# A finer, reordered work list for the convolution rounds of an S4 + SwiGLU block

## The chip, the cores and the metric

The kernel runs on one core of a Trainium2 chip. The metric is the device time of one execution in microseconds (us). The core has five engines that run their own instruction streams in order and wait for one another through semaphores: TensorE (PE, matrix products into PSUM), VectorE (DVE), ScalarE (ACT), GpSimd (POOL) and SyncE (SP, which here only issues DMA transfers). ACT and POOL issue DMA transfers too.

## The reference

The input x is 2048 rows of 640 numbers. A modulation vector (silu(c) @ w_mod) gives shifts, scales and gates. Two stages follow, each on a layer-normed and modulated copy h of x and each added back to x with a gate:

- A state-space convolution. For each of 640 channels a kernel of 2048 taps is built, K[d, l] = Re sum over n of C·exp(dt·A·l)·dt·B with 128 complex states n, and h is convolved with K causally (the reference does it with a padded FFT); Dskip·h is added.
- A SwiGLU: h @ w1 through silu, times h @ w3, all times w2, with 1728 hidden columns.

Everything is fp32.

## The kernel before, in words

**Stages.** The time falls into a front (modulation, first layer norm, first transform of u, up to about 120 us), the convolution rounds (to about 317 us), a tail of the convolution (to about 366 us), and the SwiGLU (the rest).

**The work of the rounds.** It is cut into pieces, each a small function that issues a few instructions. A piece is named by two letters and a step number, as in `T+2`. Two families run beside each other.

*Making K*: a step k makes 16 of the 640 channels, so there are 40 steps, 0 to 39.
`PH` phases as integers (three POOL operations, two steps at once), `AB`, `CO`, `SI` absolute value, cosine and sine on ACT (two steps at once), `PA` and `PQ` the exponents (PE), `XA` and `XQ` their exponentials (ACT), `E1`, `E2`, `A1`, `A2` the products of exponentials with cosines and sines (DVE, tiles E and A), `kg` the sum over the states (64 small matmuls into PSUM tile pk), `K` two DVE operations: one adds D to a column of pk (`pk<-pk,dz`), one scales pk by the gate and moves it to SBUF (`K<-pk,gaT`); `pt` a first transform of K (PE), `uk` its copy to SBUF (ACT).

*Convolving*: a step takes 4 of 32 frequencies of 128 channels (5 chunks of channels, 8 steps each). Its steps are numbered 10 to 49, so that step k of this family is worked on in the round of step k of the other.
`st` the second transform of u and K together (16 matmuls into PSUM tile p2, `p<-uk,s`), `kc` the copy of K's half (ACT), `T` two DVE products of the complex multiplication: one into an SBUF tile (`T<-p,kc`), one back into p2 (`p<-p,kc`); `Y` the difference and the sum of the products (DVE), `iv` the first inverse transform (PE, tile pz), `zt` its copy out and store (ACT and SP, every second step).

**What sets the order.** Inside the rounds every instruction of PE, DVE, ACT and POOL is held in the order in which the program issues it. That order is a string, `ROUND` (line 1028), of pieces with steps relative to the round; the loop of line 1037 goes through it for ten rounds of four steps (`EB` = 4), skipping what is done or does not exist. `do` (line 927) finds the function of a piece. A round also has, in rounds 2 to 6, one part of a late modulation product (`LS`, `LP`, `LC`, `LO`, PE and DVE). After the rounds a loop (line 1058) does the remaining convolution steps, from `st` 43 on.

DMA issues on SP are not held in that order, but SP takes them one after the other: a transfer behind one that waits is late too. The loads concerned are `s2` (in traces `s<-in_s_dram`, 256 KB, one per convolution step, two buffers), `i1`, the u of the next chunk (`uk<-us`), the stores `zs<-zt`, and, in the last rounds, `last_pair`: s2 and i1 of the last four steps, put into phase tiles that are free by then (`ph<-in_s_dram`).

**Buffers that make the pieces wait.** p2 has one PSUM place (a second one only for odd steps from 39 on), so `st` of a step waits for `Y` of the step before. PA and PQ share one place, so they alternate with XA and XQ. pk, pt and pz have one each. Phase tiles have three places: `PH` of a step waits until `A1` and `A2` of the six and five steps before it are done. The cosine tiles have two places: `AB` waits for `E1` and `E2` of four and three steps before.

Of the kernel before, what the change touches and what calls it, by code (L numbers as in the profile page):

```python
# [13 lines left out]
OP = mybir.AluOpType  # L14
# [3 lines left out]
P = 128  # L18
L = 2048
D = 640  # L20
F = 1728
NA, NB = 32, 64
DC = 128
# [3 lines left out]
NS = D // SD  # L27
EB = 4
# [13 lines left out]
def consts():  # L42
# [78 lines left out]
def tile_kernel(ctx: ExitStack, tc: tile.TileContext, a):  # L121
    nc = tc.nc
    V, S, G, PE = nc.vector, nc.scalar, nc.gpsimd, nc.tensor
# [51 lines left out]
    dz = kp.tile([P, D // 4], F32, name="dz")  # L175
# [4 lines left out]
    uk = kp.tile([P, 3, NA, DC], F32, name="uk")  # L180
# [261 lines left out]
    def late_load(i):  # L442

        late[i] = w_load(xw[:, :KD * WC].rearrange("p (k c) -> p k c", k=KD), 1920 + i * WC)
# [108 lines left out]
    ph, cs, AA, EC, PK, K1 = {}, {}, {}, {}, {}, {}  # L553
# [16 lines left out]
    def exp_slow(steps):  # L570
        exponents(pQ, steps, r1, NA)
# [65 lines left out]

    def imag2(s):
        A = AA[s]
        keep(V.scalar_tensor_tensor(A[:, :, 0, :], ph.pop(s)[:, :, 2 * NA - 1:NA - 1:-1], -1.0, A[:, :, 0, :],  # L640
                                    op0=OP.mult, op1=OP.mult))

    def tables(s):
# [3 lines left out]
    def kgen(s):  # L647
# [6 lines left out]
                                   start=(st == 0), stop=(st == 1), tile_position=(0, dq * 32)))  # L654
        PK[s] = pk

    def k1evac(s):
        dst = tp.tile([P, SD // 4, NB], F32, name="K1")
        pk = PK.pop(s)
        keep(V.tensor_tensor(pk[:, :, 0], pk[:, :, 0], dz[:, s * 4:s * 4 + 4], op=OP.add))  # L660
        keep(V.tensor_tensor(dst, pk, bc(gaT[:, s * 4:s * 4 + 4], 2, NB), op=OP.mult))
        K1[s] = dst

# [15 lines left out]
    Pq, Yq, Zq = {}, {}, {}  # L679
# [60 lines left out]
    def products(ch, g):  # L740

        p2, kc = Pq[ch, g]
        T = fp.tile([P, 2, 2, DC], F32, name="T")
        T2 = p2[:, :, :, DC:]
        keep(V.tensor_tensor(T, bc(p2[:, :, 0, :DC], 2, 2), kc, op=OP.mult))
        keep(V.tensor_tensor(T2, bc(p2[:, :, 1, :DC], 2, 2), kc[:, :, ::-1, :], op=OP.mult))
        Pq[ch, g] = (T, T2)

    def sums(ch, g):
        T, T2 = Pq.pop((ch, g))  # L750
        Y = fp.tile([P, 2, 2, DC], F32, name="Y")
        keep(V.tensor_tensor(Y[:, :, 0, :], T[:, :, 0, :], T2[:, :, 0, :], op=OP.subtract))
        last_sum[0] = keep(V.tensor_tensor(Y[:, :, 1, :], T[:, :, 1, :], T2[:, :, 1, :], op=OP.add))
        Yq[ch, g] = Y
# [101 lines left out]
    def x_tile():  # L856
        return xp.tile([P, D], F32, name="xm", bufs=6)
# [22 lines left out]
    def x_load(j):  # L880
        xe.append(xw[:, j * D:(j + 1) * D])
        nc.sync.dma_start(xe[j], a["x"][j * P:(j + 1) * P, :])
# [33 lines left out]
    def conv_part(fn):  # L916
        return lambda k: fn((k - LAG) // 8, (k - LAG) % 8)

    parts = {"PH": phases, "AB": absph, "CO": cosine, "SI": sine, "PA": lambda k: exp_fast((k,)), "XA": fast,
             "PQ": lambda k: exp_slow((k,)), "XQ": slow, "E1": real1, "E2": real2, "A1": imag1, "A2": imag2,  # L920
             "kg": kgen, "K": k1evac, "pt": k_stage1, "uk": k_out}
    conv = {"st": conv_part(stage2), "kc": conv_part(k_copy), "T": conv_part(products), "Y": conv_part(sums),
            "iv": conv_part(inverse1), "zt": conv_part(z_store)}
    by_two = ("PH", "AB", "CO", "SI")
    done = set()
# [1 line left out]
    def do(name, k):  # L927

        lo, hi = (LAG, LAG + 8 * NDC) if name in conv else (0, NS)
        if name in by_two and k % 2:  # L930
            return None
        if front[0]:
            assert (name, k) not in done and lo <= k < hi, (name, k)
        if (name, k) in done or not lo <= k < hi or (name == "zt" and k % 2 == 0 and k < LAG + 8 * NDC - 8):
            return None
        done.add((name, k))
        return (conv if name in conv else parts)[name](k)
# [72 lines left out]
    for word in FRONT:  # L1010
        name, k = word[:2].rstrip("+"), int(word[len(word[:2].rstrip("+")):])
# [14 lines left out]
    front[0] = False  # L1026

    ROUND = (
# [5 lines left out]
    ).split()  # L1034
    in_order[0] = True
    pieces = {"LS": late_sums, "LP": late_part, "LC": late_cols, "LO": late_out}
    for rnd in range(NS // EB):
        if 2 <= rnd < 7:
            late_load(rnd - 2)
        for word in ROUND:  # L1040
            name, k = word[:2].rstrip("+-"), EB * rnd + int(word[len(word[:2].rstrip("+-")):])
            if name in pieces:
                if 2 <= rnd < 7:
                    pieces[name](rnd - 2)
                continue
            do(name, k)
            if name == "iv" and 36 <= k < 40:
                with tc.issue_after(i1_last[0].ins):
                    last_pair(k - 36)
            if name == "E1" and 30 <= k < 38 and k % 2 == 0:  # L1050
                x_load((k - 30) // 2)

            if name == "kg" and 36 <= k < 40:
                early.append((None, z_tile()))
                z_load(early[-1][1], k - 36, range(3), q=nc.gpsimd)
    in_order[0] = False

    for tk in range(NS + 1, LAG + 8 * NDC + 2):
        do("st", tk)
        do("kc", tk)  # L1060
        if tk == LAG + 8 * NDC:
            end, made = late_products(6), []
            for j in (2, 3):
                py, end = x_products(j, end)
                made.append(py)
            with tc.issue_after(end.ins):
                last = do("iv", tk - 1)
        else:
            last = do("iv", tk - 1)
        do("zt", tk - 1)  # L1070
        do("T", tk)
        do("Y", tk)
        if tk == NS + 1:
            tabs.close()
            xp = ctx.enter_context(tc.tile_pool(name="xp", bufs=2))
            idle = xp.tile([P, 512], F32R, name="idle", bufs=1)
            G.memset(idle.bitcast(F32), 0.0)
            for j in range(4):
                early[j] = (x_tile(), early[j][1], xp.tile([P, KD, 6], F32, name="st5", bufs=4))
                G.memset(early[j][1][64:, :, 2 * DC:], 0.0)  # L1080
            i2bt = [h_tile() for _ in range(8 - LATE)]
        i = tk - 1 - LAG - 8 * NDC + 8
        if 0 <= i < 8:
            if i < 4:
                z_last_load = z_load(early[i][1], i, (3,), q=nc.gpsimd)
            if i == 3:
                with tc.issue_after(z_last_load.ins):
                    for t in range(8 - LATE):
                        for j in range(4):
                            nc.gpsimd.dma_start(i2bt[t][j * 32:j * 32 + 8], a["i2b"][:, t])  # L1090
            if i in (4, 5):
                x_part(i - 4, x_products(i - 4, last)[0])
            if i == 7:
                for j in (2, 3):
                    x_part(j, made[j - 2])
            if i == 6:
                pl = psS.tile([P, 2, 512], F32, name="pl", tag="A", bufs=1)
                pls += [pl[:, 0], pl[:, 1]] + [psS.tile([P, 512], F32, name="pl", tag=t, bufs=1) for t in ("pk", "pb")]
                late_products(5)
            if i == 7:  # L1100
                z_early()
                early_products()
                late_products(7)
# [22 lines left out]
    V, S, G, PE = (InOrder(tc, e, (in_order,)) for e in (nc.vector, nc.scalar, nc.gpsimd, nc.tensor))  # L1126
# [128 lines left out]
    def x_sums(i, which=range(4)):  # L1255
# [450 lines left out]
```

## Time and profile before

| | us |
|---|---|
| median of 3 runs | 929.97 |
| lowest, highest | 929.65, 930.44 |
| the profiled execution's own time | 929.82 |
| its span, first to last instruction | 927.9 |
| the T of steps 10, 14, 18, 22, 26, 30 and 34 starts at | 128.22, 155.31, 182.38, 209.45, 236.54, 263.63, 290.82 |
| the st of step 42 starts at | 335.02 |
| the last matmul of the convolution's tail ends at | about 366.2 |

The rows below are of four kinds. A row of the windows gives a stretch, its length, the busy time of PE, weight loads, DVE, ACT and POOL in it with the number of instructions, the granted TensorE clock, the DMA share and GB/s. A row of a timeline gives start, duration, engine, instruction, and in brackets how long the engine stood idle before it and for whom. A row of the chain of waits gives start, duration and what the chain went through there. All instructions of the rounds have one source line in the profile (115, a recording helper), so they are told apart by their tiles.

### The profile page before, as it was taken

The numbers are of one execution on the slowest core, as the hardware profiler recorded it, in microseconds if no ns is written. First come the engines' busy times: TensorE is split into PE (matmuls) and PEld (weight loads), VectorE is DVE, ScalarE is ACT, GpSimd is POOL, SyncE is SP. The second block draws the span as 40 slices with busy tenths as digits, with TensorE's granted clock in tenths as the row PEclk, the third lists the DMA queues.
The fourth block names the chain that finished last, engine by engine and source line by source line (L and its number), as shares of the span: only waits on it lengthen the run. The fifth ranks groups of instructions, "written<-read, shape, count | busy, mean of one in ns | idle before, by whom it ended". The sixth has DMA issues, their size and how long they took to land.

```text
span 927.9 us, 20137 instructions
## 1 busy us (share of the span) xinstructions
PE 868.2 (94%) x8082; PEld 664.7 (72%) x8082; DVE 701.6 (76%) x1210; ACT 541.6 (58%) x746; POOL 274.9 (30%) x285
## 2 busy tenths in 40 slices
PE   3788989999998899999999999999999999999997
PEld 2545566666666576678888887778888888888785
DVE  5899899999999868777666656677966666654774
ACT  5989889999999642574334323565534333333332
POOL 3333534553554222214222202310422222100331
PEclk9777689999999999999999999999999999999999
DMA  8664475676666967943122239946321311223351
GB/s 252 223 222 176 155 215 184 210 191 192 166 214 188 291 218 214 284 164 100 57 58 57 57 90 253 242 141 199 110 62 46 100 54 58 57 100 99 98 199 72
DMA packets 103328, 140.68 MB, mean 152 GB/s; under 512 B 19940, under 2 KB 62436, under 8 KB 103236
## 3 DMA queue, kind: packets, MB, share of 16 engines
q1 hardware_dynamic: 92532, 113.71, 41.0%
q10 hardware_dynamic: 8272, 18.16, 6.6%
q0 software_dynamic: 2432, 7.54, 2.5%
q8 instruction: 63, 1.03, 0.5%
q14 instruction: 29, 0.24, 0.1%
HBM read 107.92 MB, written 31.46 MB: 150 GB/s over the span
## 4 chain that ended last, share of the span: by engine, by line
PE 73%; DVE 14%; ACT 5%; DMA 4%; issue 3%; POOL 1%; SPq 0%; DVEq 0%; POOLq 0%; ACTq 0%
PE ps L115 55%; PE p L115 6%; PE pz L115 3%; PE pt L115 3%; DVE A L115 3%; DVE E L115 2%; PE pk L115 2%; DVE u L115 2%; PE pa L115 2%; DVE uk L115 1%; DMA s<-in_s_dram 1%; DVE st L115 1%; ACT A L115 1%; ACT uk L115 1%; DVE T L115 1%
## 5 line engine op out<-in xcount | busy, mean ns | idle before, releaser
L115 DVE TENSOR_TENSOR s<-ps,s 128x512 f32<-128x512 f32 x138 | 94.8, 687 | 83.2 <-PE ps L115 81.6
L115 ACT CAST gh<-rw 128x640 fp32r<-128x640 f32 x87 | 63.3, 727 | 113.4 <-PE ps L115 94.2
L115 DVE TENSOR_TENSOR gl<-rw,gh 128x640 fp32r<-128x640 f32 x87 | 78.2, 899 | 59.4 <-ACT gh L115 59.2
L115 POOL TENSOR_TENSOR S<-rw 128x256 f32<-128x256 f32 x46 | 36.2, 790 | 233.6 <-DVE S0l L115 156.2
L115 PE MATMUL ps<-xA,gh 128*128 128x512 f32 x280 | 87.9, 392 | 0.6 <-ACT xA L115 0.4
L115 PE MATMUL ps<-gh,uh 128*128 128x512 f32 x224 | 87.4, 390 | 0.0
L115 PE MATMUL ps<-gl,uh 128*128 128x512 f32 x224 | 87.3, 390 | 0.0
L115 POOL TENSOR_TENSOR ph<-thi,iota 128x1376 int32<-128x1376 int32 x20 | 51.2, 2562 | 116.1 <-DVE A L115 94.6
L115 PE MATMUL p<-uk,s 128*64 128x256 f32 x576 | 71.8, 392 | 13.5 <-DVE Y L115 3.4
L115 DVE TENSOR_TENSOR E<-A,cs 128x1024 f32<-128x1024 f32 (+1 forms) x80 | 81.0, 1024 | 2.1 <-PE pk L115 1.9
L115 PE MATMUL ps<-gh,ul 128*128 128x512 f32 x208 | 81.1, 390 | 0.0
L115 ACT ACTIVATE A<-pa 128x1024 f32<-128x1024 f32 (+1 forms) x80 | 64.2, 815 | 9.4 <-PE pa L115 8.8
L115 PEld LDWEIGHTS p<-uk,s 128*64 128x64 f32 x576 | 41.2, 139 | 35.3 <-DVE Y L115 5.7
L115 PEld LDWEIGHTS ps<-xA,gh 128*128 128x128 f32 x280 | 52.3, 188 | 13.6 <-issue 1.0
L115 DVE TENSOR_TENSOR A<-A,ph 128x1024 f32<-128x1024 f32 x40 | 54.1, 1357 | 0.8
L115 PE MATMUL ps<-xA,gl 128*128 128x512 f32 x140 | 54.5, 389 | 0.0
L115 PE MATMUL pt<-s,K 128*64 128x128 f32 x640 | 46.8, 292 | 5.4 <-ACT uk L115 5.4
L115 PEld LDWEIGHTS ps<-gh,uh 128*128 128x128 f32 x224 | 42.0, 188 | 9.0 <-DVE h L115 0.2
L115 PEld LDWEIGHTS ps<-gl,uh 128*128 128x128 f32 x224 | 42.1, 188 | 8.9
L115 ACT ACTIVATE s<-ps 128x512 f32<-128x512 f32 (+1 forms) x33 | 19.7, 597 | 47.4 <-PE ps L115 46.5
L115 PEld LDWEIGHTS pt<-s,K 128*64 128x64 f32 x640 | 37.1, 145 | 14.1 <-ACT uk L115 8.7
L115 POOL TENSOR_TENSOR rw<-rw,gbr 128x512 f32<-128x512 f32 x14 | 20.8, 1492 | 87.2 <-DMA rw<-in_w_dram 80.1
(224 smaller groups left out, 2216.0 us busy)
## 6 DMA issues: line engine op xcount, KB each, us to landing
rw<-in_w_dram ACTq DMA_DIRECT2D x44, 320.0 KB, 3.0
us<-u SPq DMA_DIRECT2D x16, 640.0 KB, 3.4
rw<-in_wg_dram SPq DMA_DIRECT2D x31, 320.0 KB, 3.0
s<-in_s_dram SPq DMA_DIRECT2D x36, 256.0 KB, 4.0
i<-in_i_dram SPq DMA_DIRECT2D x36, 256.0 KB, 4.3
rw<-in_wu_dram SPq DMA_DIRECT2D x28, 320.0 KB, 3.0
uk<-us SPq DMA_DIRECT2D x16, 512.0 KB, 6.2
zs<-zt SPq DMA_DIRECT2D x16, 512.0 KB, 5.1
```

The lines of the kernel that those rows point to most:

```text
L115: ins = fn(*args, **kw)
```

## The change

`K` is split: its first DVE operation becomes a piece of its own, `D` (function `k_direct`), and `K` calls it only if it is not yet done. `T` is split: its second product becomes the piece `P` (`products2`). `ROUND` is a new string with these pieces, and it is used for rounds 0 to 7 only; the pieces of rounds 8 and 9 stand in a second string, `LAST`, with absolute step numbers. The tail's loop calls `T`, `P` and `Y` one after the other as before. No instruction is added to the program or taken out, except that ACT's table of functions is loaded once more (30 loads before, 31 now, in the last rounds).

```diff
     def imag2(s):
         A = AA[s]
-        keep(V.scalar_tensor_tensor(A[:, :, 0, :], ph.pop(s)[:, :, 2 * NA - 1:NA - 1:-1], -1.0, A[:, :, 0, :],
+        keep(V.scalar_tensor_tensor(A[:, :, 0, :], ph[s][:, :, 2 * NA - 1:NA - 1:-1], -1.0, A[:, :, 0, :],
                                     op0=OP.mult, op1=OP.mult))
...
+    def k_direct(s):
+        pk = PK[s]
+        keep(V.tensor_tensor(pk[:, :, 0], pk[:, :, 0], dz[:, s * 4:s * 4 + 4], op=OP.add))
+
     def k1evac(s):
+        do("D", s)
         dst = tp.tile([P, SD // 4, NB], F32, name="K1")
         pk = PK.pop(s)
-        keep(V.tensor_tensor(pk[:, :, 0], pk[:, :, 0], dz[:, s * 4:s * 4 + 4], op=OP.add))
         keep(V.tensor_tensor(dst, pk, bc(gaT[:, s * 4:s * 4 + 4], 2, NB), op=OP.mult))
...
         T = fp.tile([P, 2, 2, DC], F32, name="T")
+        keep(V.tensor_tensor(T, bc(p2[:, :, 0, :DC], 2, 2), kc, op=OP.mult))
+        Pq[ch, g] = (p2, kc, T)
+
+    def products2(ch, g):
+
+        p2, kc, T = Pq[ch, g]
         T2 = p2[:, :, :, DC:]
-        keep(V.tensor_tensor(T, bc(p2[:, :, 0, :DC], 2, 2), kc, op=OP.mult))
         keep(V.tensor_tensor(T2, bc(p2[:, :, 1, :DC], 2, 2), kc[:, :, ::-1, :], op=OP.mult))
...
     ROUND = (
-        "E1+2 pt+0 CO+4 kg+1 A1+2 kc+2 SI+4 T+2 PA+4 uk+0 XA+4 Y+2 E2+2 st+3 K+1 zt+1 kc+3 A2+2 kg+2 "
...
+        "kg+1 CO+4 kc+2 E1+2 pt+0 E2+2 A1+2 PA+4 SI+4 T+2 P+2 D+1 Y+2 XA+4 A2+2 K+1 E1+3 E2+3 st+3 A1+3 A2+3 "
...
+    LAST = (
+        "CO+36 E1+34 E2+34 A1+34 kc+34 T+34 kg+33 PA+36 P+34 SI+36 Y+34 pt+32 st+35 XA+36 uk+32 E1+35 D+33 "
...
-    for rnd in range(NS // EB):
+    for rnd in range(8 + 1):
...
-        for word in ROUND:
+        for word in ROUND if rnd < 8 else LAST:
...
-        do("T", tk)
-        do("Y", tk)
+        for name in "TPY":
+            do(name, tk)
```

What the new strings move is seen in the order of the instructions on an engine.

**DVE, a steady round, products and K** (T is the first product, the second goes back into p2, Y are their sums; pk is D's addition, K1 the scaling; E and A are the products with cosine and sine; the numbers tell the buffers apart). Before:

```order
L115 TENSOR_TENSOR T_2999<-p2_2928,kc_2996 128x512
L115 TENSOR_TENSOR p2_2928<-p2_2928,kc_2996 128x4x128
L115 TENSOR_TENSOR Y_3008<-T_2999,p2_2928 128x2x128 x2
L115 TENSOR_TENSOR E_2950<-A_2771,cs_2773 128x16x32
L115 TENSOR_TENSOR pk_2962<-pk_2962,dz_77 128x4
L115 TENSOR_TENSOR K1_3024<-pk_2962,gaT_76 128x256
L115 SCALAR_TENSOR_TENSOR A_2771<-ph_2689,A_2771 128x16x32
```

Now, `D+2 T+3 K+2 P+3 Y+3 D+3` of the round, and what follows:

```order
L115 TENSOR_TENSOR pk_3035<-pk_3035,dz_77 128x4
L115 TENSOR_TENSOR T_3088<-p2_3020,kc_3077 128x512
L115 TENSOR_TENSOR K1_3090<-pk_3035,gaT_76 128x256
L115 TENSOR_TENSOR p2_3020<-p2_3020,kc_3077 128x4x128
L115 TENSOR_TENSOR Y_3137<-T_3088,p2_3020 128x2x128 x2
L115 TENSOR_TENSOR pk_3103<-pk_3103,dz_77 128x4
L115 TENSOR_TENSOR E_3144<-A_3010,cs_2808 128x16x64
```

Before, the second product stood right behind the first and K right behind D's addition; now another instruction stands between them. In a round of four steps T and its second product are neighbours four times before and twice now; the second product and Y three times before and once now; D's addition and K four times before and never now.

**ACT, a steady round, the trigonometric functions** (`cs<-ph` is AB, `cs<-cs` CO, `ph<-ph` SI, `A<-pa` XA or XQ). Before:

```order
L115 COPY kc_2451<-p2_2440 128x512
L115 ACTIVATE cs_2375<-cs_2375 128x2048
L115 COPY uk_82<-pt_2498 128x32x16
L115 ACTIVATE cs_2549<-ph_2455 128x2048
L115 ACTIVATE cs_2549<-cs_2549 128x2048
L115 COPY kc_2599<-p2_2530 128x512
L115 ACTIVATE ph_2455<-ph_2455 128x32x64
```

Now:

```order
L115 ACTIVATE cs_2352<-ph_2303 128x2048
L115 ACTIVATE A_2367<-pa_2346 128x16x2x32
L115 COPY kc_2369<-p2_2358 128x512
L115 ACTIVATE A_2367<-pa_2371 128x16x32
L115 COPY uk_82<-pt_2377 128x32x16
L115 ACTIVATE A_2393<-pa_2390 128x16x2x32
L115 ACTIVATE cs_2410<-ph_2406 128x2048
L115 ACTIVATE A_2393<-pa_2424 128x16x32
L115 ACT_TABLE_LOAD
L115 ACTIVATE cs_2352<-cs_2352 128x2048
```

The second AB of a round (`AB+8`, cs_2549 before, cs_2410 now) stood among the cosines and sines, with its own CO right behind it; now it stands ahead of the last exponential and of the table load.

**SP, the last two rounds, the loads around s2 of step 39** (the numbers tell the buffers apart). Before, s2_4175 is that load:

```order
L713 DMA ph_4084<-in_s2_dram 128x512
L790 DMA zs_58<-zt_3992 128x1024
L687 DMA uk_82<-us_57 128x8x128
L713 DMA ph_4084<-in_i1_dram 128x512
L694 DMA s2_4175<-in_s2_dram 128x512
L700 DMA i1_4267<-in_i1_dram 128x512
```

Now it is s2_4172:

```order
L717 DMA ph_4082<-in_i1_dram 128x512
L691 DMA uk_82<-us_57 128x8x128
L799 DMA zs_58<-zt_4011 128x1024
L698 DMA s2_4172<-in_s2_dram 128x512
L704 DMA i1_4246<-in_i1_dram 128x512
```

The two early loads into the phase tile now stand ahead of the u load, and the load for step 39 stands behind the store of z.

More of the change, by code (lines that the diff above doesn't have):

```diff
@@ L920, in tile_kernel @@
              "PQ": lambda k: exp_slow((k,)), "XQ": slow, "E1": real1, "E2": real2, "A1": imag1, "A2": imag2,
-             "kg": kgen, "K": k1evac, "pt": k_stage1, "uk": k_out}
-    conv = {"st": conv_part(stage2), "kc": conv_part(k_copy), "T": conv_part(products), "Y": conv_part(sums),
+             "kg": kgen, "D": k_direct, "K": k1evac, "pt": k_stage1, "uk": k_out}
+    conv = {"st": conv_part(stage2), "kc": conv_part(k_copy), "T": conv_part(products), "P": conv_part(products2), "Y": conv_part(sums),
             "iv": conv_part(inverse1), "zt": conv_part(z_store)}
@@ L1028, in tile_kernel @@
     ROUND = (
[5 rows of a table removed]
[5 rows of a table added]
+    ).split()
+    LAST = (
[8 rows of a table added]
     ).split()
@@ L1036, in tile_kernel @@
     pieces = {"LS": late_sums, "LP": late_part, "LC": late_cols, "LO": late_out}
-    for rnd in range(NS // EB):
+    for rnd in range(8 + 1):
         if 2 <= rnd < 7:
             late_load(rnd - 2)
-        for word in ROUND:
-            name, k = word[:2].rstrip("+-"), EB * rnd + int(word[len(word[:2].rstrip("+-")):])
+        for word in ROUND if rnd < 8 else LAST:
+            name, k = word.split("+")
+            k = int(k) + (EB * rnd if rnd < 8 else 0)
             if name in pieces:
```

15 rows, old and new, of tables (LAST, ROUND) are left out of this document.

## The prediction

> **What bounds the kernel now.** I read the page's first part, then a table of windows over the stretch that the change touches, then the timelines of DVE, ACT, PE and POOL in one round, then the chain of waits in the last two rounds.
>
> ```profile
> span 927.9 us, 20137 instructions
> PE 868.2 (94%) x8082; PEld 664.7 (72%) x8082; DVE 701.6 (76%) x1210; ACT 541.6 (58%) x746; POOL 274.9 (30%) x285
> ```
>
> Over the whole span PE is busy 94%, but that average is made by the SwiGLU. The stages of the change look different (columns: stretch, length, busy PE, weight loads, DVE, ACT, POOL, clock, DMA share, GB/s):
>
> ```profile
> 182.38:209.45 27.07, 25.37 (x488) 18.14 (x484) 25.52 (x42) 25.61 (x27) 13.00 (x7) 1.00 0.67 185
> 290.82:335.02 44.20, 38.72 (x805) 28.73 (x801) 38.32 (x67) 28.30 (x36) 10.26 (x17) 1.00 0.85 247
> 335.02:366.19 31.17, 31.17 (x467) 21.76 (x465) 23.81 (x59) 11.13 (x21) 8.41 (x16) 1.00 0.69 215
> ```
>
> The first row is one round, from one T of a round to the next. It lasts 27.07 us, and three engines have nearly the same work in it: ACT 25.61, DVE 25.52, PE 25.37. None is full; each stands idle about 1.5 us because of the other two. So the round cannot go below about 25.5, and what an order can win is at most 1.5 us a round. The second row is the last two rounds, up to the st of step 42: PE has 38.72 of 44.20 us, the others less, so up to 5.5 us are waits. The third row is the tail, where PE is busy all the time; its order does not change, so it only starts earlier.
>
> Where DVE's 27.07 us go is in its timeline:
>
> ```profile
> 182.38 0.69 DVE L115 TENSOR_TENSOR T<-p,kc 128x512 f32<-128x512 f32 x1 [1.08 <-ACT kc L115]
> 183.11 0.70 DVE L115 TENSOR_TENSOR p<-p,kc 128x512 f32<-128x512 f32 x1
> 183.84 0.75 DVE L115 TENSOR_TENSOR Y<-T,p 128x256 f32<-128x256 f32 x2
> 184.51 0.69 DVE L115 TENSOR_TENSOR E<-A,cs 128x512 f32<-128x512 f32 x1
> 185.11 0.17 DVE L115 TENSOR_TENSOR pk<-pk,dz 128x4 f32<-128x4 f32 x1
> 185.31 0.42 DVE L115 TENSOR_TENSOR K<-pk,gaT 128x256 f32<-128x256 f32 x1
> 185.65 0.68 DVE L115 SCALAR_TENSOR_TENSOR A<-ph,A 128x512 f32<-128x512 f32 x1
> ...
> 193.52 1.69 DVE L115 TENSOR_TENSOR A<-A,ph 128x1024 f32<-128x1024 f32 x1
> 195.13 0.16 DVE L115 TENSOR_TENSOR pk<-pk,dz 128x4 f32<-128x4 f32 x1
> 195.32 0.42 DVE L115 TENSOR_TENSOR K<-pk,gaT 128x256 f32<-128x256 f32 x1
> 195.66 1.22 DVE L115 TENSOR_TENSOR E<-A,cs 128x1024 f32<-128x1024 f32 x1
> 196.80 0.69 DVE L115 TENSOR_TENSOR T<-p,kc 128x512 f32<-128x512 f32 x1
> ...
> 202.33 0.15 DVE L115 COPY modT<-pm 128x3 f32<-128x3 f32 x1
> 202.40 0.68 DVE L115 SCALAR_TENSOR_TENSOR A<-ph,A 128x512 f32<-128x512 f32 x1
> ```
>
> I count from start to start. An E of 0.69 is followed 0.60 later by an instruction that does not need it (184.51 to 185.11). A T of the same 0.69 is followed 0.73 later by p (182.38 to 183.11), which works in the same tile and waits for it; p is followed 0.73 later by Y, which reads it. D's addition is followed by K 0.20 later, the equally small modT copy by a stranger 0.07 later. So an instruction right behind the one that it needs costs about 0.12 us more than elsewhere. Beside that the round has one wait of 1.08 for kc, and an A that takes 1.69 (it meets the POOL operation at 194.21, quoted under D), 0.47 more than the 1.22 of an E of its size.
>
> **The change part by part.** *Spacing on DVE.* Eight such neighbours go per round: two of T and p, two of p and Y, four of D and K. At 0.12 each that is 0.96 us; the additions now slip into the shadow between p and Y twice, which costs nothing new. DVE's round without its wait is 27.07 - 1.08 = 25.99, and becomes 25.0. The cost of the A at 1.69 stays in this number, since two phases per round remain to meet DVE. Bounds: nothing (if the spacing is worth nothing) to 1.5 (if the slow A's are met by a wait instead). I take 0.96.
>
> *ACT's round.* DVE alone cannot shorten the round, since ACT has 25.61 of work.
>
> ```profile
> 189.06 0.59 ACT L115 COPY uk<-pt 128x512 f32<-128x512 f32 x1 [0.18 <-PE pt L115]
> 190.84 0.59 ACT L115 COPY uk<-pt 128x512 f32<-128x512 f32 x1 [0.27 <-PE pt L115]
> 192.67 1.03 ACT L115 ACTIVATE A<-pa 128x1024 f32<-128x1024 f32 x1 [0.75 <-PE pa L115]
> 193.59 1.91 ACT L115 ACTIVATE cs<-ph 128x2048 f32<-128x2048 int32 x1
> 195.40 0.59 ACT L115 ACTIVATE A<-pa 128x512 f32<-128x512 f32 x1
> ...
> 205.08 1.93 ACT L115 ACTIVATE cs<-ph 128x2048 f32<-128x2048 int32 x1
> 207.04 1.91 ACT L115 ACTIVATE cs<-cs 128x2048 f32<-128x2048 f32 x1
> 208.86 0.57 ACT L115 COPY kc<-p 128x512 f32<-128x512 f32 x1
> ```
>
> Its waits are for PE: 0.18, 0.27, 0.75. An AB takes 1.81 to the next start when a stranger follows (193.59 to 195.40) and 1.96 when its own CO does (205.08 to 207.04); the new order parts the two, 0.15 won. I laid the new round out on paper with the start-to-start times of these rows (AB, CO, SI 1.82, XA 0.92, XQ, kc, uk 0.5, zt 0.9, a table load 1.4 with the gap ahead of it), starting at CO+4: the table load for the exponentials begins at 4.2, AB+6 at 10.85, AB+8 at 16.6, the load for the sines at 19.1, CO+6 at 20.4, SI+6 at 24.1, and the next CO+4 at 25.9. What waits are left there are short: 0.1 at XQ+5, 0.2 at kc+4 and 0.5 at uk+2, all for PE, whose matmul groups I placed at 1.88 for st, 1.09 for iv, 1.03 for pt and 1.11 for kg. In this layout DVE is ready for T+5 at 21.3 and kc+5 ends at 22.8: the wait for kc has not gone, it has moved from T+2 to T+5, and ACT is now last. Next late is PE: st+3 must begin 4.7 after CO+4, and PE finishes the work ahead of it at just that point.
>
> The round becomes 26.0 (25.9 and 0.1 for what paper forgets). The six rounds from the T of step 10 (128.22) to that of step 34 (290.82) took 162.60 us, 27.10 on average:
>
> ```profile
> 128.22 0.69 DVE L115 TENSOR_TENSOR T<-p,kc 128x512 f32<-128x512 f32 x1
> ...
> 290.82 0.68 DVE L115 TENSOR_TENSOR T<-p,kc 128x512 f32<-128x512 f32 x1
> ```
>
> 6 x (27.10 - 26.0) = 6.6 us. Bounds: ACT's own 25.6 gives 9.0; no gain gives 0. Rounds 0 and 1 are mostly done by the front and count for nothing.
>
> *The last two rounds.* The chain of waits there:
>
> ```profile
> 309.83 0.92 SPq L713
> 310.81 9.52 DMA s<-in_s_dram
> 320.37 1.95 PE p L115 x16
> ```
>
> The st of step 39 waited for its s2, which took 9.52 us to land because the DMA engines were full. The row of 290.82 to 335.02 has a share of 0.85 with 37.6 us of transfers (0.85 x 44.20). Laid out the same way from T+34 at 0, the new list runs DVE without a wait to about 28, PE is the next limit, and st of step 42 starts at 39.6, close to PE's own 38.72. In this layout s2 of step 39 can be issued at 17.5, behind the store of z of step 35, and is wanted at 25.4: 7.9 us, 1.6 less than the 9.52 that it took before. I add these 1.6: 41.2 instead of 44.2, a gain of 3.0. Bounds: 38.7, PE's work, gives 5.5; if transfers alone decide, the gain is 0, or below it. The table load added here costs 1.4 on ACT, which has 28.30 of work in 44.20 and hides it.
>
> *Sum.* 929.82 - 6.6 - 3.0 = 920.2 for the profiled execution; the median of the runs is 0.15 above it: 920.4.
>
> One rule speaks against the first term. The row: 0.60 behind an E against 0.73 behind a T. The Trainium skill (VectorE: DVE Perf Modes, The DRAIN you can't avoid) says that the next operation does not start until the pipe is empty, semaphore or not, so chaining costs nothing extra; the same section adds that an operation that is not held starts earlier. By its first sentence the spacing would be worth 0, by the row 0.96 a round. The trace is with the second.
>
> **The rivals.** *A, spacing is worth nothing.* Then DVE stays at 25.99 without waits, and a round comes out between that and 27.07, in the middle at 26.5: 6 x 0.6 = 3.6; with half of the last rounds' 3.0 the time is 929.97 - 5.1 = 924.9. For it: T and p read PSUM and an E does not, which could make the 0.13 by itself. Against it: D and K, 0.20 against 0.07, where both first instructions work on a few columns of PSUM. This is the case of the skill's rule above.
>
> *B, the last rounds belong to the DMA engines.* Their 37.6 us of transfers are in order behind SP, and faster rounds only bring them closer together. Then only 6.6 is won: 923.4. For it: a share of 0.85 already. Against it: the loads wait for buffers that now come free earlier.
>
> *C, the waits only change place.* PE's 25.37 with one more wait of 1.5 makes 26.9, and the last rounds win 0.5: 929.97 - 1.2 - 0.5 = 928.3, about no change. For it: three engines within 0.25 us of each other.
>
> *D, slower: the phases come too late for AB+8.*
>
> ```profile
> 190.79 0.69 DVE L115 SCALAR_TENSOR_TENSOR A<-ph,A 128x512 f32<-128x512 f32 x1
> 191.63 2.50 POOL L115 TENSOR_TENSOR ph<-thi,iota 128x1376 int32<-128x1376 int32 x1 [8.87 <-DVE A L115]
> 194.21 1.50 POOL L115 TENSOR_TENSOR ph<-ph,phi 128x256 int32<-128x256 int32 x1
> 195.79 2.54 POOL L115 TENSOR_TENSOR ph<-ph 128x768 int32<-128x768 int32 x1
> ```
>
> A phase starts when DVE releases its tile (191.48, POOL at 191.63) and ends 6.7 later (198.33); AB read it at 205.08, so 6.75 us of cover. In the new round PH+8 can start when A2+3 is done, at 9.1, ends at 15.8, and AB+8 wants it at 16.6: 0.8 of cover. Behind AB+8 stand XQ+7, the table load and all sines, for which DVE waits. If A2+3 comes L later, the round is 26.0 + (L - 0.8); the whole is slower once 6 x (L - 0.8 - 1.1) exceeds 3.0, at L = 2.4. With L = 3 it is 929.97 + 6 x 1.1 - 3.0 = 933.6. For it: the cover shrinks from 6.75 to 0.8. Against it: A2+3 is waited for by nothing but DVE's own order, and DVE has slack there.
>
> **How the numbers follow.** The forecast has 0.60, A 0.10, B 0.13, C 0.08, D 0.09. The forecast's own range is 917 to 923.5. The range 916 to 927.5 holds nearly all of the forecast with A and B, and leaves out C, D and little else. What a measurement of this kernel tells from no change is about 0.2%, 1.9 us. Faster by more: 0.60 + 0.10 + 0.13 = 0.83; within: C, 0.08; slower: D, 0.09.
>
> **What would show it.** Right: starts of every fourth T 26.0 apart; behind T, K starts 0.60 later; DVE's wait for kc ahead of T+5, not of T+2; ACT busy over 98% of a round; st of step 42 about 41 us after the T of step 34; the tail unchanged at 31.2 us. A is shown by p 0.6 behind a K and the round yet unshortened in DVE's busy time; B by an st of the last rounds that waits for a DMA for more than 3 us; C by new PE waits; D by an AB that waits for POOL. I am wrong if the rounds stay at 27, or if the tail or the SwiGLU change by more than 1 us.

## The result, and the profile after

The changed kernel takes 939.95 us (median; 938.83 to 941.34), the kernel before 929.87 us on the same chip: a ratio of 1.0101, with a 95% interval of 1.0079 to 1.0122. It is slower by about 10 us where 9.5 us of gain were forecast, outside the range.

The spans of the two profiled executions are 939.6 and 927.9 us, 11.7 apart. Windows of the changed kernel, cut at the same instructions as before (stretch, length, busy PE, weight loads, DVE, ACT, POOL, clock, DMA share, GB/s):

```profile
187.91:216.41 28.50, 26.71 (x498) 19.21 (x490) 26.23 (x43) 25.14 (x27) 10.68 (x6) 0.94 0.61 174
216.41:244.96 28.55, 26.75 (x544) 19.51 (x532) 28.04 (x44) 26.88 (x27) 11.54 (x6) 1.00 0.68 201
301.47:346.63 45.16, 41.52 (x802) 31.05 (x791) 36.66 (x66) 29.28 (x37) 10.28 (x17) 0.92 0.83 247
346.63:377.80 31.17, 31.17 (x467) 21.76 (x465) 23.79 (x59) 11.52 (x21) 8.40 (x16) 1.00 0.67 209
```

The first two rows are two rounds: 28.5 us each where 26.0 were forecast and 27.1 stood before. The T of step 10 starts at 130.19 (before: 128.22), that of step 34 at 301.47, the st of step 42 at 346.63. So 1.97 us are lost ahead of the T of step 10, 8.68 in the six rounds (171.28 against 162.60), 0.96 in the last two rounds, nothing in the tail: 11.61 together.

DVE, which had work for about 25.5 us of a round, now has 26.2 and 28.0. Its groups over the six rounds say which instructions grew. First the kernel before, then the changed one (count, busy time, mean ns of one, idle time before):

```profile
L115 DVE TENSOR_TENSOR A<-A,ph 128x1024 f32<-128x1024 f32 x24 | 34.5, 1439 | 0.6
L115 DVE TENSOR_TENSOR E<-A,cs 128x1024 f32<-128x1024 f32 x24 | 30.0, 1250 | 0.0
L115 DVE TENSOR_TENSOR E<-A,cs 128x512 f32<-128x512 f32 x24 | 16.4, 684 | 0.0
L115 DVE SCALAR_TENSOR_TENSOR A<-ph,A 128x512 f32<-128x512 f32 x24 | 16.4, 683 | 0.0
```

```profile
L115 DVE TENSOR_TENSOR A<-A,ph 128x1024 f32<-128x1024 f32 x25 | 33.0, 1324 | 0.0
L115 DVE TENSOR_TENSOR E<-A,cs 128x1024 f32<-128x1024 f32 x24 | 31.8, 1323 | 0.0
L115 DVE SCALAR_TENSOR_TENSOR A<-ph,A 128x512 f32<-128x512 f32 x24 | 22.4, 934 | 0.6
L115 DVE TENSOR_TENSOR E<-A,cs 128x512 f32<-128x512 f32 x24 | 21.8, 908 | 0.0
```

The small products E2 and A2 grew from 0.68 to 0.91 and 0.93 us. (The 25th A1, `A<-A,ph`, of the changed kernel is one of 2.61 us that begins at 127.66, ahead of the six rounds; without it the mean is 1270 ns.) The timelines of DVE and POOL in one round of the changed kernel show what they met (first DVE, then POOL):

```profile
193.83 0.69 DVE L115 SCALAR_TENSOR_TENSOR A<-ph,A 128x512 f32<-128x512 f32 x1
194.43 0.16 DVE L115 TENSOR_TENSOR pk<-pk,dz 128x4 f32<-128x4 f32 x1
194.50 0.68 DVE L115 TENSOR_TENSOR T<-p,kc 128x512 f32<-128x512 f32 x1
195.10 0.41 DVE L115 TENSOR_TENSOR K<-pk,gaT 128x256 f32<-128x256 f32 x1
195.43 0.69 DVE L115 TENSOR_TENSOR p<-p,kc 128x512 f32<-128x512 f32 x1
196.15 0.75 DVE L115 TENSOR_TENSOR Y<-T,p 128x256 f32<-128x256 f32 x2
196.82 0.16 DVE L115 TENSOR_TENSOR pk<-pk,dz 128x4 f32<-128x4 f32 x1
196.89 2.40 DVE L115 TENSOR_TENSOR E<-A,cs 128x1024 f32<-128x1024 f32 x2
199.39 1.90 DVE L115 SCALAR_TENSOR_TENSOR A<-ph,A 128x512 f32<-128x512 f32 x1
```

```profile
194.66 2.50 POOL L115 TENSOR_TENSOR ph<-thi,iota 128x1376 int32<-128x1376 int32 x1 [9.49 <-DVE pk L115]
197.24 1.50 POOL L115 TENSOR_TENSOR ph<-ph,phi 128x256 int32<-128x256 int32 x1
198.82 1.92 POOL L115 TENSOR_TENSOR ph<-ph 128x768 int32<-128x768 int32 x1
```

The spacing works as forecast: K starts 0.60 behind T, T 0.07 behind D's addition, Y 0.72 behind p. But the A at 199.39, an instruction of 0.69 like the one at 193.83, takes 1.90: it ends 0.55 after POOL's third operation (198.82 to 200.74). E1 and E2 ahead of it (196.89, two instructions of 1.22 and 0.69, 1.81 in a row where nothing is in the way) take 2.40. T, K, p and Y beside POOL's first operation keep their times. In the kernel before, POOL's third operation ran beside T, p and Y (195.79 to 198.33 there), and one A of the phase, that of 1.69 at 193.52, was held up.

The size of such a loss can be read from the rows: a product that is held up takes longer by what the POOL operation running at its start still has to run, less 0.13 us. The A at 199.39 starts 1.35 ahead of the end of the third operation and takes 1.22 longer than 0.68. The A at 193.52 of the kernel before starts 0.61 ahead of the end of POOL's first operation (191.63 to 194.13) and takes 0.47 longer than 1.22. All 42 products that lost time in the six rounds of the two kernels fit this to 0.01 us.

The 1.97 us ahead of the T of step 10 are a loss of this kind too. There the kernel before has one E and one A between D's addition (at 124.02) and T:

```profile
124.56 1.94 DVE L115 TENSOR_TENSOR E<-A,cs 128x1024 f32<-128x1024 f32 x1
126.61 1.48 DVE L115 TENSOR_TENSOR A<-A,ph 128x1024 f32<-128x1024 f32 x1
```

The changed kernel, whose addition starts at 123.47, has E2 there as well (first DVE, then POOL):

```profile
124.02 3.72 DVE L115 TENSOR_TENSOR E<-A,cs 128x1024 f32<-128x1024 f32 x2
127.66 2.61 DVE L115 TENSOR_TENSOR A<-A,ph 128x1024 f32<-128x1024 f32 x1
```

```profile
123.10 2.50 POOL L115 TENSOR_TENSOR ph<-thi,iota 128x1376 int32<-128x1376 int32 x1 [6.44 <-ACT cs L115]
125.69 1.51 POOL L115 TENSOR_TENSOR ph<-ph,phi 128x256 int32<-128x256 int32 x1
127.27 1.92 POOL L115 TENSOR_TENSOR ph<-ph 128x768 int32<-128x768 int32 x1
```

E1 and E2 lose 1.91 there and A1 1.40, against 0.72 and 0.26 before. From the addition to T it is 6.72 us instead of 4.20. PE meanwhile stands idle for 4.46 us until Y is done, and the st that follows (132.49) takes 3.68 us instead of 1.95, at a granted clock of 0.50 in the 4 us from 132. The first of the six rounds takes 29.21 us.

The chain of waits of the changed kernel in the last two rounds:

```profile
319.08 11.22 DMA s<-in_s_dram
330.30 0.14 issue
330.44 1.94 PE p L115 x7
```

The s2 of step 39 was issued 17.6 after the T of step 34 (forecast 17.5), but took 11.22 us to land, not less than the 9.52 of before. PE stood only 0.83 us for it (1.19 before), since it had come late itself: its work in the last two rounds took 41.52 us at a granted clock of 0.92, where 38.72 at 1.00 had been enough, and 2.64 us went in a stop that is shown below.

### The profile page after: what moved, and what is told of

It is laid out like the page before. It is cut to its first block, busy times and chain, and to the rows that moved or that the text cites. A ratio compares the mean times of both kernels' runs of the same rounds, so it can differ in the third digit from the quotient of the medians.

```text
span 939.6 us, 20133 instructions
## 1 busy us (share of the span) xinstructions
PE 874.8 (93%) x8082; PEld 669.6 (71%) x8082; DVE 708.4 (75%) x1210; ACT 542.6 (58%) x747; POOL 262.6 (28%) x285
## 4 chain that ended last, share of the span: by engine, by line
PE 70%; DVE 16%; ACT 7%; DMA 4%; issue 3%; POOL 0%; SPq 0%; DVEq 0%; ACTq 0%; POOLq 0%
PE ps L115 55%; PE p L115 5%; DVE E L115 4%; DVE A L115 4%; ACT cs L115 2%; PE pt L115 2%; PE pu L115 2%; PE pz L115 2%; PE pk L115 2%; DVE Y L115 1%; DVE T L115 1%; DMA s<-in_s_dram 1%; DVE p L115 1%; DVE uk L115 1%; ACT A L115 1%
## 5 line engine op out<-in xcount | busy, mean ns | idle before, releaser
L115 PE MATMUL p<-uk,s 128*64 128x256 f32 x576 | 77.6, 415 | 13.4 <-issue 9.0
L115 DVE TENSOR_TENSOR E<-A,cs 128x1024 f32<-128x1024 f32 (+1 forms) x80 | 87.5, 1125 | 2.7 <-PE pk L115 1.7
L115 PEld LDWEIGHTS p<-uk,s 128*64 128x64 f32 x576 | 43.7, 147 | 37.3 <-issue 16.2
L115 DVE TENSOR_TENSOR A<-A,ph 128x1024 f32<-128x1024 f32 x40 | 51.1, 1283 | 0.0
L115 PE MATMUL pk<-E 128*32 128x64 f32 x1280 | 44.5, 235 | 4.3 <-issue 2.6
L115 PEld LDWEIGHTS pt<-s,K 128*64 128x64 f32 x640 | 39.3, 149 | 12.8 <-ACT uk L115 5.7
```

The lines of the kernel that those rows point to most:

```text
L115: ins = fn(*args, **kw)
```

## The experiments

All times are medians beside the kernel before on the same chip; "a round" is the mean of the five rounds from the T of step 14 to that of step 34, "last" the time from there to the st of step 42, both from the trace of one execution. That execution is not always near the median (924.2 against 919.28 with quiet POOL, 934.5 against 930.77 with spacing only). The kernel before took 929.5 to 930.6 us on the chips of the experiments; the ratios are to that.

| kernel | us | ratio to before (95%) | a round | last |
|---|---|---|---|---|
| before | 929.87 | 1 | 27.10 | 44.20 |
| changed | 939.95 | 1.0079 to 1.0122 | 28.41 | 45.16 |
| new rounds, old last rounds | 938.29 | 1.0074 to 1.0108 | 28.37 | 43.87 |
| old rounds, new last rounds | 930.29 | 0.9993 to 1.0030 | 27.22 | 44.34 |
| changed, quiet POOL | 919.28 | 0.9873 to 0.9928 | 25.78 | 44.74 |
| before, quiet POOL | 929.27 | 0.9990 to 1.0012 | 27.08 | 44.48 |
| changed, phases in windows | 925.38 | 0.9928 to 0.9979 | 26.56 | 44.82 |
| changed, tables later | 939.04 | 1.0082 to 1.0123 | 28.41 | 44.72 |
| windows and tables later | 925.21 | 0.9934 to 0.9972 | 26.52 | 42.01 |
| before, spacing only | 930.77 | 0.9981 to 1.0015 | 27.32 | 45.59 |
| windows, kc early | 926.55 | 0.9932 to 0.9975 | 26.68 | 44.22 |
| windows, kc early, tables later | 924.92 | 0.9923 to 0.9957 | 26.76 | 41.74 |
| changed, more PE instructions | 937.19 | one time | 28.38 | 43.44 |

### Which of the two strings loses

The string of rounds 8 and 9 is replaced by the old order (cut into the same finer pieces), or that of rounds 0 to 7 is. The first of the two edits, cut:

```diff
     LAST = (
-        "CO+36 E1+34 E2+34 A1+34 kc+34 T+34 kg+33 PA+36 P+34 SI+36 Y+34 ... Y+41 iv+40 st+42 iv+41 "
+        "E1+34 pt+32 CO+36 kg+33 A1+34 kc+34 SI+36 T+34 P+34 PA+36 uk+32 ... Y+41 st+42 iv+41 AB+44 "
```

> The new order for the eight rounds, the old order (in fine parts) for the last two. The changed kernel lost 1.97 us before the T of step 10, 8.68 in the six rounds to the T of step 34, 0.96 in the last two rounds. Main theory (the phase operations of POOL now run beside E and A, which read two operands in SBUF, and one blocks the other): the rounds keep their 28.5 us, all the loss in them stays, 938 to 940. Rival 'the last rounds belong to the transfers' says no more than 1 us here: 939. Rival 'the order of the last rounds upsets the whole': near 930.

> The old order for the eight rounds, the new order for the last two. Main theory: the rounds take 27.1 us again. If the last two rounds are worth what the prediction gave them where they are not fed by disturbed rounds, 927; if their s2 of step 39 is late whatever came before, 930 to 931 (as in the changed kernel, 0.96 lost).

938.29 and 930.29 us. The rounds lose about 9 us by themselves, the new order of the last rounds neither wins nor loses more than the measurement can tell.

### POOL that reads nothing

From step 12 on the three operations of a phase become two memsets (the output is then not the reference's), in the changed kernel and in the kernel before:

```diff
-        hold(G.tensor_tensor(p[:, :, b0:], bc(thi...), bc(iota...), op=OP.mult))
-        keep(G.tensor_tensor(base, base, bc(phi...), op=OP.add))
-        keep(G.tensor_tensor(p[:, :, :b0]..., bc(base...), bc(p[:, :, NPH:]...), op=OP.add))
+        keep(G.memset(p, 0))
+        keep(G.memset(p, 0))
```

> The changed kernel, with the three phase operations of POOL from step 12 on replaced by two memsets of the phase tile to zero (the tables are then wrong, so the output is not the reference's): they only write, read nothing in SBUF, and take about as long. Main theory: E2 and A2 take 0.69 again instead of 0.9 on average, DVE's round falls to about 25.2, rounds to 26.0 to 26.5 instead of 28.5 from the T of step 14 on, 927 to 930 in all (five rounds won by 2.0 to 2.5). Rival 'phases come too late for AB+8': the release and the time of the phase are much the same, rounds stay near 28. Rival 'PE pauses halve its clock': rounds stay near 28 and the clock below 0.95.

> The kernel before, with the same two memsets in place of the phase operations from step 12 on (output not the reference's). Main theory: there the collisions cost a round about 0.5 to 1 us (the A of 1.69): rounds 26.3 to 26.8 instead of 27.1, 926 to 928.5. If the collisions cost nothing in either kernel: 930.

The changed kernel falls from 939.95 to 919.28 us, more than was expected, and 1.1 us from the forecast. The kernel before stays at 929.27: the gain expected there did not come. Groups of the changed kernel with memsets, over its five rounds, and one of its rounds:

```profile
L115 DVE TENSOR_TENSOR E<-A,cs 128x1024 f32<-128x1024 f32 x20 | 24.3, 1214 | 0.0
L115 DVE TENSOR_TENSOR A<-A,ph 128x1024 f32<-128x1024 f32 x20 | 24.2, 1215 | 0.0
L115 DVE SCALAR_TENSOR_TENSOR A<-ph,A 128x512 f32<-128x512 f32 x20 | 13.7, 683 | 0.5
L115 DVE TENSOR_TENSOR E<-A,cs 128x512 f32<-128x512 f32 x20 | 13.7, 683 | 0.0
L115 POOL MEMSET ph<- 128x2144 int32 x20 | 37.7, 1887 | 90.7 <-DVE pk L115 47.2 <-DVE A L115 42.9
```

```profile
207.73:233.52 25.79, 25.23 (x496) 18.17 (x488) 24.53 (x44) 25.31 (x27) 7.55 (x4) 1.00 0.70 208
```

Every product has one time, 1.21 or 0.68. Against these, four instructions of each of the four kinds per round lost 4 x (0.225 + 0.036 + 0.001) = 1.0 us to POOL in the kernel before (the A1, E1 and E2 groups; A2 lost nothing) and 4 x (0.055 + 0.109 + 0.251 + 0.225) = 2.6 us in the changed one (A1 with the mean of 1270). The first loss does not matter: with it gone, the old order still takes 27.08, and DVE waits 8.5 us for kc in five rounds where it waited 5.0. From D's addition to the T of step 10 the changed kernel with memsets takes 4.20 us again. The waits of ACT over the six rounds (total, times, longest) of the kernel before with memsets are the same 5.0 and 2.9 us as without them:

```profile
ACT A L115 <- PE pa L115: 5.0, 7, 0.7
ACT uk L115 <- PE pt L115: 2.9, 12, 0.4
```

The changed kernel with memsets has one such line over its five rounds, the changed kernel itself waits for DVE too:

```profile
ACT uk L115 <- PE pt L115: 1.7, 5, 0.3
```

```profile
ACT A L115 <- PE pa L115: 8.9, 6, 4.8
ACT cs L115 <- DVE E L115: 6.2, 5, 1.3
ACT kc L115 <- PE p L115: 3.9, 8, 1.3
```

So the old round is set by ACT and PE, whatever DVE loses. With the new order those waits are gone once POOL is quiet, and DVE's loss shows in full: 2.63 us a round between the changed kernel with and without memsets. Two memsets take 3.8 us, a phase alone 4.7, so a phase also ends about 1 us earlier here. That this is not the cause is seen in the changed kernel itself, where AB waits for E and not for POOL, and in the next run.

The memset edit leaves the time of the profiled execution at 924.2, while the other executions of this kernel took 918.2 to 919.3. Its trace thus shows 5 us less of gain than the median, and where the other executions saved these is not seen. What the trace does show is a gain in the rounds alone: 156.02 us for the six, where 162.60 stood before.

### Phases in windows

The whole computation again. The second operation of a phase (and the third behind it) waits for the last E or A ahead of a T, and some pieces of DVE, ACT and PE change places (cut):

```diff
-        keep(G.tensor_tensor(base, base, bc(phi[:, sl], 2, 8), op=OP.add))
+        add = keep(G.tensor_tensor(base, base, bc(phi[:, sl], 2, 8), op=OP.add))
+        if in_order[0] and s >= 14:
+            tc.add_manual_dep(add.ins, free[s].ins.name,
...
+                              reason="phase behind products")
...
-        "... Y+2 XA+4 A2+2 K+1 ... PH+8 AB+8 K+3 P+4 LS+4 A2+5 LP+4 PQ+7 iv+3 Y+4 LC+4 A1+4 XQ+7 LO+4 A1+5 CO+6 st+5 ..."
+        "... Y+2 XA+4 K+1 A2+2 ... PH+8 PQ+7 K+3 XQ+7 P+4 LS+4 Y+4 LP+4 iv+3 A2+5 LC+4 A1+4 LO+4 A1+5 CO+6 AB+8 st+5 ..."
```

> The changed kernel with its whole computation, but each phase of POOL cut in two: the first operation still runs beside T and P of step 3 (or 5) of a round, the second and third wait for E2+5 (or A1+2) and so run beside T, P, Y of step 4 (or 2). On DVE Y+4 and K+1 stand ahead of A2+5 and A2+2, on ACT AB+8 stands behind CO+6. Main theory (one operation of POOL that reads SBUF shuts out a DVE product of two operands in SBUF until it ends, and the other way round): no E or A takes over 1.35, rounds 25.8 to 26.3, 918.5 to 922. Rival 'phases come too late for AB+8': they end later here than in the changed kernel, so rounds of 28 or more, over 938. Rival 'any activity of POOL slows DVE': nothing won, 938 to 941.

925.38 us: faster than both kernels, though not all of what was expected. POOL in one round:

```profile
209.12 0.65 POOL L115 TENSOR_TENSOR ph<-ph,phi 128x256 int32<-128x256 int32 x1 [4.46 <-DVE A L115]
209.85 1.60 POOL L115 TENSOR_TENSOR ph<-ph 128x768 int32<-128x768 int32 x1
215.82 2.50 POOL L115 TENSOR_TENSOR ph<-thi,iota 128x1376 int32<-128x1376 int32 x1 [4.37 <-DVE pk L115]
222.69 0.64 POOL L115 TENSOR_TENSOR ph<-ph,phi 128x256 int32<-128x256 int32 x1 [4.36 <-DVE E L115]
223.40 1.60 POOL L115 TENSOR_TENSOR ph<-ph 128x768 int32<-128x768 int32 x1
```

The second and third operations now take 0.65 and 1.60 in every round, where they took 1.09 and 1.93 on average in the changed kernel, and the products have 0.68 and 1.22 to 1.25 again. POOL does the same work as in the changed kernel, and its phases end later after their release (AB+8, which reads them, stands later too). So POOL's activity as such did not make the changed kernel slow, nor did late phases, for which AB did not wait there: it was which DVE instruction stood beside which POOL operation. The Trainium skill (SBUF — State Buffer, Who interferes with whom) states just this: a VectorE instruction with two SBUF inputs contends with a GpSimd instruction that reads SBUF, not with one that only writes, whoever starts first holds the port for the whole instruction, and an instruction with one SBUF input is left alone. The trace agrees: 0.68 against 1.90 for A2, 0.65 against 1.50 for the addition of phi, and no change for T, p and Y.

A round takes 26.4 us in four of the five rounds and 27.3 in the fifth, instead of 25.8. DVE waits 7.3 us for kc ahead of the five T+5, since AB+8 now stands between CO+6 and kc+5 on ACT; but with quiet POOL it waits 6.3 there as well. ACT waits 2.4 us for pa, for which it did not wait with quiet POOL. Which of these makes the 0.6 us is not shown.

### The order on ACT

Against phases in windows, zt+3 and kc+5 move ahead of AB+8 (cut):

```diff
-        "... CO+6 AB+8 st+5 pt+3 kc+5 zt+3 T+5 P+5 kg+4 uk+3 ..."
+        "... CO+6 st+5 pt+3 zt+3 kc+5 AB+8 T+5 P+5 kg+4 uk+3 ..."
```

> Phases in windows, and on ACT after CO+6 the order zt+3, kc+5, AB+8, uk+3 instead of AB+8, kc+5, zt+3, uk+3. In the run of phases in windows no product was held up any more, and a round took 26.4 instead of the 25.8 of quiet phases: DVE waited 1.2 for kc at T+5 (behind AB+8), ACT 0.5 for pa. Theory 'ACT's own order holds the round': T+5 comes 0.6 earlier, the wait of iv for zt goes, 26.1 to 26.4 a round, and the step into the last rounds (6.45 from T of step 33 to T of step 34, against 5.5 elsewhere) shortens by 0.5 to 1: 922.5 to 925. If ACT is full whatever its order, 925.

926.55 us and 26.68 a round: nothing won. T+5 waits 0.6 to 1.2 us for kc instead of 1.2 to 2.1, but DVE now waits 0.98 for kc ahead of every T+2 from step 14 on, and PE 0.88 for Y ahead of an st. The expectation that ACT's own order holds the round is not borne out by this order of it.

### The last two rounds

The eight loads into phase tiles (s2 and i1 of steps 42 to 45, not of the last four, 46 to 49) are issued two steps later, in the changed kernel and in the two kernels with windows:

```diff
-            if name == "iv" and 36 <= k < 40:
+            if name == "iv" and 38 <= k < 42:
                 with tc.issue_after(i1_last[0].ins):
-                    last_pair(k - 36)
+                    last_pair(k - 38)
```

> The changed kernel, with the eight loads into the phase tiles (tables of steps 42 to 45, 2 MB) issued two steps later each, behind iv of steps 38 to 41 instead of 36 to 39. Theory 'the transfers ahead of it make s2 of step 39 late': s2 of step 39 lands in 8 us or less, its st loses its wait and its half clock, from T of step 34 to st of step 42 42 us instead of 45.2, 936 to 937.5. Rival 'PE halts by itself there': 45 us again, 939 to 941.

> The two edits together. If both theories hold and are independent: the gain of the first (about 20) and of the second (3): 915.5 to 918. If the second gives nothing, the time of the phases in windows alone.

> The same with the eight loads of tables two steps later. The profiled executions differed by 2.8 us in the last two rounds, the medians by 0.2: if the profiled execution was typical, 2 to 3 us less than the run without the later loads; if not, the same within 1 us.

With windows the st of step 39 no longer waits for its s2, and the last two rounds take 42.01 and 41.74 us instead of 44.82 and 44.22. The medians fall by 0.2 and by 1.6 us, both within the intervals, so a gain is not shown by them, and the 915.5 to 918 expected of both edits was missed with the first. In the changed kernel itself s2 of step 39 lands in 7.5 us and its st no longer waits for it, as the theory said; yet the edit brings nothing (939.04; last rounds 44.72), as its rival said: there PE stops by itself. PE in the changed kernel, at kg of step 37:

```profile
324.93 0.29 PE L115 MATMUL pk<-A 128*32 128x64 f32 x8
325.04 0.28 PE L115 MATMUL pk<-E 128*32 128x64 f32 x4
327.96 0.25 PE L115 MATMUL pk<-E 128*32 128x64 f32 x2 [2.64 <-issue]
```

The stop of 2.64 us comes in the middle of a run of matmuls with the same operands, after the 52nd of 64, and the profile shows nothing that it waits for. In the kernel with quiet POOL and in that with later tables it comes after the same 52nd matmul (1.65 and 2.72 us), in that with old rounds and new last ones after the 51st (1.75), in those with windows after the 56th (1.25 to 2.00).

> The changed kernel, with the 8 matmuls of pt of step 30 written three times over (same operands, same result): 16 matmuls more ahead of the last rounds. In the changed kernel and three of its variants PE stops for 1.6 to 2.7 us after the 52nd of the 64 matmuls of kg of step 37, which waits for nothing. Theory 'PE has run out of instructions there, and the stop belongs to a place in its instruction stream': it now stops after the 36th of the 64. Rival 'something that this group waits for, which the profile does not show': still after the 52nd.

```diff
-        for g in range(4):
+        for g in [0, 1, 2, 3] * (3 if s == 30 else 1):
```

The stop after the 52nd is gone, in the one execution of this kernel. The expectation counted wrongly: one matmul of the program is two in the trace (8114 PE instructions against 8082), so the place moved by 32, to the 20th. There the rows do change, without a stop:

```profile
323.37 0.29 PE L115 MATMUL pk<-A 128*32 128x64 f32 x8
323.48 0.42 PE L115 MATMUL pk<-E 128*32 128x64 f32 x6
323.67 0.25 PE L115 MATMUL pk<-A 128*32 128x64 f32 x2
```

The matmuls, issued in steady runs of 8 until then, come in twos and fours from the 20th on, as they do behind the stop in the changed kernel. So the place belongs to PE's instruction stream and not to what kg waits for. When the instructions come late is seen in the packets of the instruction queue, q8. In the eight kernels that stop, the last packet starts from 0.1 us behind to 1.1 us ahead of the last matmul before the stop, and PE goes on 2.3 to 2.8 us after that packet started. In this run the packet starts 2.5 us ahead of the 20th matmul (321.04), and the 21st comes 2.6 us after it. In the four kernels without a stop the matmul of the same count comes 4.1 to 5.3 us after its packet. So every trace fits a stop that lasts until the packet is in; why a packet is late was not tried. Without the stop, the st of step 39 waits 3.04 us for its s2 here, so that the last two rounds still take 43.44. The Trainium skill (Runtime: NRT & Kernel Launch, Instruction fetch mechanics) states that an engine fetches its instructions in blocks of 256 by its own DMA queue, and that this is mostly hidden. The queue q8 agrees with the size (63 packets for 16164 matmuls and weight loads, 257 each); that the fetch was hidden does not hold in these rounds, where the DMA share reached 1.04.

### Spacing alone

The old order on ACT, PE and POOL, with D, P and K moved on DVE. Of the eight dependent neighbours that the new order parts in a round, this parts six (cut):

```diff
-        "... PA+4 uk+0 XA+4 Y+2 ... E2+3 K+2 ... st+4 PA+7 K+3 ... zt+3 T+4 LS+4 Y+4 ..."
+        "... PA+4 uk+0 XA+4 D+1 Y+2 ... E2+3 D+2 K+2 ... st+4 PA+7 D+3 ... zt+3 T+4 K+3 P+4 LS+4 E2+4 Y+4 ..."
```

> The old order on ACT, PE and POOL in all rounds, and only DVE's neighbours parted (an E or A between T and P, P and Y, D and K). The first term of the forecast as it stood (spacing worth 0.96 us of DVE a round, 8 rounds): 26.1 to 26.6 a round, 924 to 926. Rival, from the run of the kernel before with quiet phases, which took DVE's collisions away and won nothing: DVE's work does not set the old round, the order on ACT does: 27.0 to 27.1 a round, 929 to 931.

930.77 us. In its round from 183.13 on, DVE still has 25.66 us of work of 27.08, since an E now meets POOL (1.59 instead of 1.22; over five rounds POOL costs DVE 1.4 us a round, 1.1 before), and ACT waits for PE as before (0.18, 0.27 and 0.74 in this round). The first term of the forecast is worth nothing by itself. Whether it is worth anything together with ACT's new order is open: no run has that order without the spacing.

## Why the prediction was wrong

- **The step that failed** is the sentence "The cost of the A at 1.69 stays in this number, since two phases per round remain to meet DVE". It took the cost of meeting POOL as a property of the phases, 0.47 for an A, and named the wrong operation: this A did not wait for the one at 194.21 but for the end of the one at 191.63, and held up the one at 194.21 (1.50 instead of 0.65). The cost is one of the pairing: 1.0 us a round with T, p and Y beside the third operation, 2.6 us with E1, E2 and A2 beside the second and third. The release of PH+8 by A2+3 was moved on paper (to 9.1), but not which products stand 2.5 to 5 us behind it. These 1.6 us a round made DVE last, where the forecast had ACT last, and what hung on it followed: AB+8 waits up to 1.3 for E2+5 (5 times, 6.2 us), since the cosine tiles are held, and PE waits 1.35 for the copy of xw in four of the six rounds. The bounds of this term, "nothing to 1.5", left out a loss, though the A of 1.69 was in the quoted rows.
- **A term put at nothing** is the sentence "Rounds 0 and 1 are mostly done by the front and count for nothing". The T of step 10 came 1.97 late, by the same pairing: 2.52 more from D's addition to T, with an addition 0.55 earlier.
- **The layout of ACT was right.** Without the collisions a round takes 25.78 (forecast 26.0), and in it AB+6, AB+8 and the next CO+4 begin 10.83, 16.57 and 25.79 after CO+4 (forecast 10.85, 16.6 and 25.9). The wait for kc did move to T+5. That the whole then takes 919.28, near the 920.4 of the forecast, is luck as far as the trace shows: the profiled execution, at 924.2, wins the 6.6 of the rounds and none of the 3.0 of the last two rounds (44.74).
- **The spacing on DVE was right as a size** (0.60, 0.07), but not as a term: alone it gave nothing. The reason that rival A gave, that a start behind a T takes 0.73 whatever follows, is refuted by 0.60; that the spacing is worth nothing, as it said, is what the run of it alone showed.
- **The last two rounds** were forecast at 41.2 and took 45.16. The issue of s2 came when forecast; the landing was taken as 9.52 and took 11.22, and with the st at half clock (3.68 instead of 1.95) and a stop of PE of 2.64, which the layout did not have, the gain was gone. Rival B had the right mechanism in part only. Its sign, an st that waits over 3 us for a DMA, was not there (0.83). With later tables the wait went; the last rounds then took 41.7 to 42.0 in the kernels with windows, but 44.72 in the changed kernel, where PE still stopped. All these are times of single executions.
- **Rival D** had the right sign by another mechanism: its late phases did not hold AB+8, which waited for E. With windows the phases end later still, and the kernel is faster than before.
- **Rival C** had a sign right, new waits of PE (1.35 for xw), but not the time, no change.
- **The tail** stayed at 31.17, as forecast.
- **Open**: what moves the start of the rounds from kernel to kernel. D's addition ahead of the T of step 10 starts between 122.51 and 124.87 in the traces looked at, and with quiet POOL the T is still 0.85 late. Nor was it tried why a PE packet is late, which of the other places of AB+8 is best, or what the spacing is worth in the new order.

## What to carry to other kernels

Before an order is changed, list for each POOL operation which DVE instructions will stand beside it, and how many of their operands lie in SBUF: here a product of two SBUF tiles and a POOL operation that reads SBUF ran one after the other, and one with an operand in PSUM ran beside it free of cost. The operations of a POOL phase can be made to wait for the start of such a free stretch one by one; here that, with AB and a few other pieces moved, turned 1% slower into 0.5% faster with the same work. A saving on one engine is worth testing alone: here neither the spacing on DVE nor the quiet POOL gave anything in the old order; what quiet POOL saved there went into DVE's wait for kc.

## What was not expected of the hardware

Behind the pause of 4.46 us ahead of 132.49 the granted clock of PE was 0.50 (132 to 136). But it also fell in rounds where PE had paused for only 1.35 us. Windows of 4 us in the changed kernel:

```profile
204.00:208.00 4.00, 2.65 (x20) 1.87 (x20) 4.00 (x8) 3.97 (x4) 0.00 (x0) 0.77 0.93 287
208.00:212.00 4.00, 4.00 (x94) 2.93 (x92) 1.91 (x3) 2.69 (x5) 3.15 (x2) 0.80 0.24 59
```

Behind that pause an st took over 2.8 us instead of 1.95, while a pause of 1.58 in the kernel before (314.09) left the clock at 1.00. The Trainium skill (TensorE: Matmul & The Clock Gate, What's actually happening) gives about 3.4 us of idle time for the fall to half clock; the clock fell here with a shorter pause, so what else counts is open. No run was made on this.
